# Stacked left-over rows for groups 4 to 15, held in the place of the split rows, and group 3's main feature matmuls ahead of group 1's second transform

## Chip, core and metric

The kernel runs on one core of one Trainium2 chip. The metric is the device time of one execution in microseconds (us), the median of three runs. A core has TensorE (PE: the matmuls; PEld: its weight loads), VectorE (DVE), ScalarE (ACT), GpSimd (POOL) and SyncE (SP), which issues most of the DMAs. Sixteen DMA engines carry out what the queues issue.

## What is computed

A spectral filter with a residual, and after it a bilinear gated layer with a residual. The change lies in the first half of the filter, the two-dimensional forward transform.

```python
def _A_ref(x, w_r, w_i):                     # x is 1 x 2048 x 640
    X = rfft2(x, axes=(-2, -1))
    X = X * (w_r + 1j * w_i)                 # w is 2048 x 321
    return irfft2(X, s=(S, D), axes=(-2, -1))

def _B_ref(x, w_gate, w_up, w_down):         # 640 -> 1728 -> 640
    g = einsum("bsd,df->bsf", x, w_gate)
    u = einsum("bsd,df->bsf", x, w_up)
    return einsum("bsf,fd->bsd", g * u, w_down)

x = A_x
h = x + _A_ref(_layernorm(x), A_w_r, A_w_i)
out = h + _B_ref(_layernorm(h), B_w_gate, B_w_up, B_w_down)
```

## The kernel before

The transforms are matmuls with constant tables. A first stage over 16 row tiles (to about 38 us) folds and normalises the rows and leaves the first transform in `s1` (four parts of 128 rows) and `rest` (128 left-over rows), both ordered by 16 groups of 128 columns. `rest_split` writes the left-over rows as a rounded high part (ACT, L281) and the remainder (DVE, L282) into `s1r`.

The second stage (about 40 to 111 us) is a loop over the 16 groups. For a group, `d_mm` makes the feature transform on PE: four main matmuls of full fp32 precision and then the left-over rows. Of a plain group these are six matmuls of 322 columns (high by high, high by low, low by high, for `re` and `im`). Of a group in `ST` they are four matmuls of 160 to 194 columns, whose stationary tile has 99 rows: the high rows, the low rows and the high rows again, 33 each, stacked. `d_out` copies the PSUM banks to `t` (ACT, L437 to L440). `s2_mm` makes the second transform into the PSUM tile `u`, of which there is one. `filt` multiplies by the filter (DVE, L455 to L458; the first three read `u`). `is2_mm` starts the inverse, and `is2_out` copies it away (ACT L506 and L517, DVE L524, POOL).

[...] `spread` writes 33 rows of `s1r` for a run of groups to `sfar` in DRAM (four DMAs, L422), and `stack` reads them back as 99 rows for two or three groups (two DMAs, of 66 and of 33 rows, L429). Groups 5 to 14 are stacked, by four stacks in two buffers (`dC`, `qt`) in turn; groups 0 to 4 and 15 are plain.

Each group also needs a load set: `load_wm` (the 128x256 tile `m` of the second transform from `in_mm_dram` L385, the 128x644 filter `wre` L386 and for even groups, which fetch it for two, `wim` L388) and `load_wi` (a second 128x256 tile L393). The tiles have three places by `g % 3`, so a set is issued three groups ahead, when the readers of its place are done.

The order is written out by hand (`manual_schedule`), each engine works in program order, and all the DMAs named here are issued by SP, one after another: one that has to wait holds up those behind it. In iteration `g`, the order is `s2_mm(g)`, `d_mm(g+2)`, `is2_mm(g-1)`, `filt(g)`, `load_wm(g+3)`, `d_out(g+2)`, `is2_out(g-1)`, `load_wi(g+2)`. Ahead of the loop stand the load sets of groups 0, 1 and 2, the spread of groups 5 to 9, and `d_mm` and `d_out` of groups 0 and 1. From about 111 us on come the inverse feature transform and the gated layer, on PE nearly without a gap.

Of the kernel before, what the change touches and what calls it, by code (L numbers as in the profile page):

```python
# [11 lines left out]
F32 = mybir.dt.float32  # L12
F32R = mybir.dt.float32r
# [3 lines left out]
P = 128  # L17
S, D, NF, FF = 2048, 640, 321, 1728
NT = S // P
NG = 16  # L20
# [4 lines left out]
RROWS = ((31, 1), (0, 1), (62, 2), (63, 2))  # L25
RWHERE = ((1, 0), (0, 0), (1, 160), (0, 160))
RW = (160, 194, 162, 162)
PLAIN, LAST = 5, 15
IPLAIN, IFAR = 6, 10
SUMS = 7  # L30
IPARTS = ((6, 4), (10, 3), (13, 3))
AGAIN = {0: (5, 3), 1: (8, 2, "qt"), 5: (10, 3), 7: (13, 2, "qt")}
NR = 4
AHEAD = 5
FOLDS = {0: (1, 2), 1: (3,), 2: (4,), 7: (9,), 9: (11,)}
# [11 lines left out]
def f32(ap):  # L47
    return ap.bitcast(F32)
# [29 lines left out]
def tile_spectral_glu(ctx: ExitStack, tc: tile.TileContext, x, wre, wim, wgu, wlast, wdown, wdlast,  # L78
# [6 lines left out]
    far = ctx.enter_context(tc.tile_pool(name="far", bufs=1, space=bass.MemoryType.DRAM))  # L85
# [13 lines left out]
    def bank(tag, bufs=2):  # L99
        return pools["y" if tag in ("im2", "ir2") else "a"].tile([P, 512], F32, tag=tag, name=tag, bufs=bufs)  # L100
# [10 lines left out]
    def wk(shape, name):  # L111
        return work.tile(shape, F32, tag="wk", name=name)
# [4 lines left out]
    def mmx(o, l, r, start, stop):  # L117
        nc.tensor.matmul(o, l, r, start=start, stop=stop, skip_group_check=True)  # L118
# [13 lines left out]
    def home(tag, shape, name, dt=F32):  # L132
        return keep.tile(shape, dt, tag=tag, name=name)

    def cut(t, o, *shape):
        v = t[:, o:o + int(np.prod(shape))]
        names = [f"d{i}" for i in range(len(shape))]
        return v.rearrange(f"p ({' '.join(names)}) -> p {' '.join(names)}", **dict(zip(names[1:], shape[1:])))
# [6 lines left out]
    s1r = home("wA", [P, 2, NG, P], "s1r", F32R)  # L145
# [127 lines left out]
    def s1_rest(t):  # L273
        act(at(rest, t), PS1[t][1][:, 0:P].rearrange("p (g m) -> p g m", g=32), AF.Copy)

    def s1_main(t, ps, a, b):
        act(view(s1, 4 * t + 2048 * a, [[2048, b - a], [64, 32], [1, 4]]),
            ps[:, a * P:b * P].rearrange("p (c g m) -> p c g m", c=b - a, g=32), AF.Copy)

    def rest_split(a, b):  # L280
        act(s1r[:, 0, a:b], rest[:, a:b], AF.Copy)  # L281
        tt(s1r[:, 1, a:b], rest[:, a:b], f32(s1r[:, 0, a:b]), op=OP.subtract)  # L282

    banks("y", "pinv")
# [30 lines left out]
    for t in range(NT):  # L315
        if t == 1:
            nc.gpsimd.dma_start(frall, frem)
        if t >= 1:
# [18 lines left out]
            if t < AHEAD - 1:  # L337
                s1_rest(t - 1)
                main = lambda: s1_main(t - 1, PS1[t - 1][0], 0, 4)
# [25 lines left out]
        else:  # L365
            scale_c(0)
            b2a, b2, b3a, a2, b3, a3, m, v = stats[0]
# [6 lines left out]
        s1_mm(t)  # L374
    s1_main(NT - 1, PS1[NT - 1][0], 2, 4)
    s1_rest(NT - 1)
    for a, b in ((0, 2), (2, PLAIN), (PLAIN, PLAIN + 5), (PLAIN + 5, 13), (13, 16)):
        rest_split(a, b)

    WM, WI = {}, {}  # L380

    def load_wm(g):
        m, w, j = mts[g % 3], wts[:, g % 3], g // 2 if g < NG - 2 else g - 7
        i = wts[:, 5 if j == 8 else 3 + j % 2]
        nc.sync.dma_start(m, mm[g, :, 0])  # L385
        nc.sync.dma_start(w, wre[g])  # L386
        if g % 2 == 0 or g >= NG - 2:
            nc.sync.dma_start(i, wim[j])  # L388
        WM[g] = (m, w, i)

    def load_wi(g):
        WI[g] = wis[g % 3]
        nc.sync.dma_start(WI[g], mm[g, :, 1])  # L393

    qm = home("qm", [P, 4, NT, P], "qm")
    qr = home("qr", [P, 2, NT, P], "qr", F32R)
    PD, T, PU, Y, PI = {}, {}, {}, {}, {}

    def parts(ps, main, rest):
        for k, (b, o, w, l, r) in enumerate(main):  # L400
            mmx(ps[b][:, o:o + w], l, r, k < 2, False)
        for k, (b, l, r) in enumerate(rest):
            mmx(ps[b][:, 0:NQ], l, r, False, k >= len(rest) - 2)

    def d_mm(g):
        ps = PD[g] = bank("re"), bank("im")
        where = ((1, 0), (0, 0), (1, 160), (0, 160))
        main = [(b, o, FW[c], s1[:, c, g], fmt[:, FOFF[c]:FOFF[c] + FW[c]]) for c, (b, o) in enumerate(where)]
        if g not in ST:
            parts(ps, main, [(b, s1r[:, k, g], frt[:, l, b]) for k, l in ((0, 0), (0, 1), (1, 0)) for b in range(2)])  # L410
            return
        parts(ps, main, [])
        for q, ((b, o), w) in enumerate(zip(RWHERE, RW)):
            a = 4 * NQ + sum(RW[:q])
            mmx(ps[b][:, o:o + w], ST[g][0:99, q], frall[0:99, a:a + w], False, q >= 2)

    ST = {}
    sfar = far.tile([4, 2, 33, LAST - PLAIN, P], F32, name="sfar")

    def spread(a, b):  # L420
        for q, (r, s) in enumerate(RROWS):
            nc.sync.dma_start(sfar[q, :, :, a - PLAIN:b - PLAIN].rearrange("l r g n -> r l g n"),  # L422
                              f32(s1r[r:r + 32 * s + 1:s, :, a:b]))

    def stack(g, n, tag="dC"):
        o = home(tag, [P, 4, n, P], "st", F32R)
        src = sfar[:, :, :, g - PLAIN:g - PLAIN + n].rearrange("q l r g n -> q (l r) (g n)")
        for a, b, r in ((0, 66, 0), (66, 99, 0)):
            nc.sync.dma_start(f32(o[a:b].rearrange("p q g n -> p q (g n)")),  # L429
                              src[:, r:r + b - a].rearrange("q r n -> r q n"))  # L430
        for i in range(n):
            ST[g + i] = o[:, :, i]

    def d_out(g):
        ps = PD[g]
        t = T[g] = wk([P, 2, NQ], "t")
        act(t[0:64, 0], ps[0][0:64, 0:NQ], AF.Copy)  # L437
        act(t[0:64, 1], ps[0][64:128, 0:NQ], AF.Copy)
        act(t[64:128, 0], ps[1][0:64, 0:NQ], AF.Copy)
        act(t[64:128, 1], ps[1][64:128, 0:NQ], AF.Copy)  # L440

    def s2_mm(g):
        if g >= NG - 2:
            ps = PU[g] = bank("re"), bank("im")
        else:
            PU[g] = pools["y"].tile([P, 2, 512], F32, tag="u", name="u", bufs=1)
            ps = PU[g][:, 0], PU[g][:, 1]
        for h in range(2):
            nc.tensor.matmul(ps[h][:, 0:NQ], WM[g][0][:, h], T[g][:, h], start=True, stop=True)  # L449
# [10 lines left out]
    def filt_half(g, h, alone=False):  # L460
        if h == 0:
            Y[g] = wk([P, 2, NQ], "y"), wk([P, 2, NQ], "us")
        y, us = (a[:, h] for a in Y[g])
        v, w, im = PU[g][h][:, 0:NQ], WM[g][1], WM[g][2]
        direct = lambda: tt(y, v, w[:, h], op=OP.mult)
        join = lambda: tt(y, y, us, op=OP.add)
        if alone:
            direct()
            nc.vector.scalar_tensor_tensor(us[0:64], v[64:128], -1.0, im[64:128, h], op0=OP.mult, op1=OP.mult)
            tt(us[64:128], v[0:64], im[0:64, h], op=OP.mult)  # L470
            return direct, join
        act(us[0:64], v[64:128], AF.Copy, scale=-1.0)
        act(us[64:128], v[0:64], AF.Copy)
        nc.gpsimd.tensor_tensor(us, us, im[:, h], op=OP.mult)
        return direct, join
# [55 lines left out]
        main(slice(0, 4))  # L531
        edges(nc.gpsimd)

    for g in range(3):
        load_wm(g)
        load_wi(g)
    spread(PLAIN, PLAIN + 5)
    d_mm(0)
    d_out(0)
    d_mm(1)  # L540
    d_out(1)
    for g in range(NG - 1):
        s2_mm(g)
        if g + 2 < NG:
            d_mm(g + 2)
        if g >= 5 and g in AGAIN:
            stack(*AGAIN[g])
        if g + 3 == NG:
            xt = home("big", [P, 2, 5, 2, 512], "xt", F32R)
            flat = xt[:, 1].rearrange("p k l n -> p (k l n)")  # L550
            irt, sirt = cut(flat, 0, 5, NQ), cut(flat, 5 * NQ, 4, 162)
            scrap, near = cut(flat, 2258, D), cut(flat, 2258 + D, 4, 4, P)
        if g == NG - 2:
            nc.gpsimd.dma_start(flat[:, 0:2258], irem)
        if g == NG - 2:
            s2_mm(g + 1)
            filt_half(g, 0, True)
            is2_out(g - 2)
        if g >= 1:
            is2_mm(g - 1)  # L560
        if g < NG - 2:
            filt(g)
        else:
            late = [filt_half(g, 1), filt_half(g + 1, 0), filt_half(g + 1, 1, True)]
            for f in (late[0][0], late[1][0], late[1][1], late[2][1]):
                f()
        if g + 3 < NG:
            load_wm(g + 3)
        if g + 2 < NG:
            d_out(g + 2)  # L570
        if g >= 1:
            if g != NG - 3:
                is2_out(g - 1)
            if g + 2 < NG:
                load_wi(g + 2)
        if g < 2:
            stack(*AGAIN[g])
        elif g == 2:
            spread(PLAIN + 5, LAST)
        if g == 6:  # L580
            nc.sync.dma_start(cit, ci)
            nc.sync.dma_start(imt, imain)
# [248 lines left out]
    for ts in (range(3), range(3, 6), range(6, 8)):  # L831
        n, t0 = len(ts), ts[-1] + 1
# [660 lines left out]
```

## Time and profile before

| | |
|---|---|
| median of 3 runs | 681.81 us (681.48 to 682.31) |
| the profiled execution | 682.02 us, its span 680.2 us |
| PE busy | 668.6 us, 98% of the span |
| DVE / ACT / POOL busy | 472.5 / 322.0 / 392.0 us |
| HBM read / written | 54.20 / 10.57 MB |

The span is what the trace covers; the execution's own time lies 1.8 us above it. Times in the rows are counted from the span's start. A busy share is an average over stages with different limits, so a change in one stage is read from the rows of that stage. A wait is put down to the event that came last in the record, which need not be the one that was waited for.

### The profile page before, as it was taken

To read this page: it belongs to the slowest core of one execution; us is meant where nothing else is said; L and a number is where in the kernel's file an instruction comes from. 1 tells how busy PE (TensorE), PEld (TensorE's weight loads), DVE (VectorE), ACT (ScalarE), POOL (GpSimd) and SP (SyncE) were. 2 spreads that over 40 slices of the span, in tenths; PEclk is the share of its full clock that TensorE was granted. 3 is DMA by queue.
4 is the path that set the end of the run, shared out by engine and by line. 5 is a ranking of instruction groups with operands and counts; after the bars stand their busy time and mean duration, and the time that the engine had idled before them with its cause. 6 is when DMAs were issued, how large, how long until landed. Compare 5 with 4: busy or idle time off the path is not lost.

```text
span 680.2 us, 10297 instructions
## 1 busy us (share of the span) xinstructions
PE 668.6 (98%) x3714; PEld 591.2 (87%) x3714; DVE 472.5 (69%) x966; ACT 322.0 (47%) x623; POOL 392.0 (58%) x376
## 2 busy tenths in 40 slices
PE   8999999999999999999999999999999999999997
PEld 8988888887888888888888889888888888888887
DVE  7968887787965958576767747854747575756654
ACT  6966665476534434352525336543434252524220
POOL 3101123642099787876987634199687878787610
PEclk9999999999999999999999999999999999999999
DMA  9537965502111102133242449201112121212003
GB/s 333 205 104 242 270 192 164 145 28 78 52 49 58 48 28 78 40 97 79 77 93 82 99 87 296 82 21 49 49 39 78 40 78 39 78 40 79 1 1 154
DMA packets 49085, 65.44 MB, mean 96 GB/s; under 512 B 24086, under 2 KB 31326, under 8 KB 48906
## 3 DMA queue, kind: packets, MB, share of 16 engines
q1 hardware_dynamic: 48314, 62.23, 29.7%
q0 software_dynamic: 288, 2.16, 0.9%
q8 instruction: 29, 0.48, 0.3%
q10 hardware_dynamic: 432, 0.39, 0.2%
q14 instruction: 22, 0.18, 0.1%
HBM read 54.20 MB, written 10.57 MB: 95 GB/s over the span
## 4 chain that ended last, share of the span: by engine, by line
PE 93%; DMA 3%; DVE 2%; ACT 1%; issue 1%; ACTq 0%; SPq 0%; DVEq 0%
PE e L118 50%; PE d L118 26%; PE eo L118 3%; PE u L449 3%; PE re L118 2%; PE im L491 2%; PE im L118 2%; PE y L118 2%; DMA tab<-in_fmain_dram 1%; PE im L251 1%; PE ir L491 1%; DMA x<-in_x_dram 1%; DMA cct<-in_cc_dram 1%; DMA wts<-in_wre_dram 0%; PE u L491 0%
## 5 line engine op out<-in xcount | busy, mean ns | idle before, releaser
L118 PE MATMUL e<-xt,wst 128*128 128x512 f32 x864 | 213.3, 391 | 0.7 <-ACT c L1076 0.7
L118 PEld LDWEIGHTS e<-xt,wst 128*128 128x128 f32 x864 | 159.8, 188 | 31.5 <-ACT c L1076 0.9
L1011 DVE TENSOR_TENSOR x<-d,x 128x320 f32<-128x320 f32 x280 | 123.4, 484 | 51.6 <-PE d L118 47.4
L118 PE MATMUL d<-wd,ht 128*128 128x320 f32 x832 | 143.6, 308 | 0.0
L118 PEld LDWEIGHTS d<-wd,ht 128*128 128x128 f32 x832 | 131.1, 188 | 7.6
L118 PE MATMUL e<-t,wst 128*128 128x512 f32 x360 | 94.3, 392 | 0.0
L925 POOL TENSOR_TENSOR wst<-raw,wst 128x1024 fp32r<-128x1024 f32 x23 | 55.5, 2411 | 66.3 <-ACT wst L924 55.8
L118 PEld LDWEIGHTS e<-t,wst 128*128 128x128 f32 x360 | 66.3, 188 | 12.6
L118 PE MATMUL d<-wt,ht 128*128 128x320 f32 x360 | 69.5, 310 | 0.0
L941 POOL TENSOR_TENSOR wst<-raw,wst 128x896 fp32r<-128x896 f32 (+1 forms) x46 | 65.1, 1439 | 3.3 <-ACT wst L936 3.3
L118 PEld LDWEIGHTS d<-wt,ht 128*128 128x128 f32 x360 | 57.3, 188 | 2.4
L1027 ACT ACTIVATE ht<-e 128x512 fp32r<-128x512 f32 x44 | 26.3, 598 | 47.5 <-DVE e L1090 23.3
L936 ACT ACTIVATE wst<-raw 128x896 fp32r<-128x896 f32 (+1 forms) x48 | 30.2, 676 | 31.7 <-POOL raw L930 30.9
L1066 ACT ACTIVATE h<-e 128x512 f32<-128x512 f32 x24 | 14.3, 596 | 64.2 <-PE e L118 64.2
L520 POOL CAST qr<-bits 1x128 fp32r<-1x128 f32 x15 | 4.2, 282 | 69.7 <-DVE qr L524 69.7
L986 DVE TENSOR_TENSOR x<-d,x 128x320 f32<-128x320 f32 x62 | 27.5, 485 | 23.2 <-PE d L118 22.9
L118 PE MATMUL e<-xt,wdir 128*128 128x512 f32 x180 | 42.3, 393 | 0.1
L627 ACT ACTIVATE wd<-draw 128x320 fp32r<-128x320 f32 (+1 forms) x30 | 15.7, 558 | 54.6 <-POOL draw L637 51.4
L1086 DVE TENSOR_TENSOR e<-e,h 128x512 f32<-128x512 f32 x24 | 16.8, 699 | 33.9 <-PE e L118 24.2
L118 PEld LDWEIGHTS e<-xt,wdir 128*128 128x128 f32 x180 | 33.4, 188 | 7.8 <-issue 0.6
L1030 DVE TENSOR_TENSOR ht<-e,ht 128x512 fp32r<-128x512 f32 x54 | 37.0, 686 | 1.6 <-ACT ht L1027 1.3
L606 POOL TENSOR_TENSOR wd<-draw,wd 128x640 fp32r<-128x640 f32 x8 | 12.5, 1580 | 40.8 <-ACT wd L605 40.8
(224 smaller groups left out, 1205.8 us busy)
## 6 DMA issues: line engine op xcount, KB each, us to landing
raw<-in_wgu_dram SPq DMA_DIRECT2D x24, 640.0 KB
draw<-in_wdown_dram SPq DMA_DIRECT2D x24, 320.0 KB
wts<-in_wre_dram SPq DMA_DIRECT2D x16, 322.0 KB
x<-in_x_dram SPq DMA_DIRECT2D x15, 320.5 KB
out_dram<-x SPq DMA_DIRECT2D x15, 320.0 KB
bits<-in_mm_dram SPq DMA_DIRECT2D x32, 128.0 KB
wts<-in_wim_dram SPq DMA_DIRECT2D x9, 322.0 KB
zfar<-zr SPq DMA_DIRECT2D x32, 80.0 KB
```

Source lines behind the costliest of these rows:

```text
L118: nc.tensor.matmul(o, l, r, start=start, stop=stop, skip_group_check=True)
L449: nc.tensor.matmul(ps[h][:, 0:NQ], WM[g][0][:, h], T[g][:, h], start=True, stop=True)
L491: nc.tensor.matmul(out, y[:, h, a:b], inv(g, h), start=n == 0, stop=n == len(ys) - 1)
L627: act(o[:, 0, a:a + n], src, AF.Copy)
L925: ptt(wa[:, 1], stage[:, 0:1024], f32(wa[:, 0]), op=OP.subtract)
L936: act(ws[:, 0, o:o + b - a], stage[:, a:b], AF.Copy)
L941: ptt(ws[:, 1, o:o + b - a], stage[:, a:b], f32(ws[:, 0, o:o + b - a]), op=OP.subtract)
L986: tt(xv, ps[b][:, 0:320], xv, op=OP.add)
L1011: tt(xv, o, xv, op=OP.add)
L1027: act(hop[:, a, 0], src, AF.Copy)
L1030: engine.tensor_tensor(hop[:, a, 1], src, f32(hop[:, a, 0]), op=OP.subtract)
L1086: tt(ob, ob, h1, op=OP.add)
```

## The change

Groups 4 to 15 are stacked. The first spread covers groups 4 to 8, the second 9 to 15. There are five stacks: groups 4 to 6 (`dC`), 7 and 8 (`qt`), 9 to 11 and 12 to 14 (both inside `s1r`, in the place of the split rows that have been spread), and 15 (`qt`). They are issued ahead of the loop and in iterations 0, 3, 5 and 7. The split of groups 9 to 15 moves from ahead of `d_out(0)` to behind `d_out(1)` on ACT and behind `filt(0)` on DVE. Group 2's load set is issued behind the first spread instead of ahead of it. On PE the main matmuls of group 3 move from behind `s2_mm(1)` to ahead of it.

```diff
-PLAIN, LAST = 5, 15
+PLAIN, MID = 4, 9
...
-AGAIN = {0: (5, 3), 1: (8, 2, "qt"), 5: (10, 3), 7: (13, 2, "qt")}
+AGAIN = {0: (7, 2, "qt"), 3: (9, 3, 0), 5: (12, 3, 1), 7: (15, 1, "qt")}
...
-    def rest_split(a, b):
+    def rest_high(a, b):
         act(s1r[:, 0, a:b], rest[:, a:b], AF.Copy)
+
+    def rest_low(a, b):
         tt(s1r[:, 1, a:b], rest[:, a:b], f32(s1r[:, 0, a:b]), op=OP.subtract)
...
-    for a, b in ((0, 2), (2, PLAIN), (PLAIN, PLAIN + 5), (PLAIN + 5, 13), (13, 16)):
-        rest_split(a, b)
+    for a, b in ((0, 2), (2, PLAIN), (PLAIN, MID)):
+        rest_high(a, b)
+        rest_low(a, b)
...
-    qr = home("qr", [P, 2, NT, P], "qr", F32R)
...
-    def d_mm(g):
-        ps = PD[g] = bank("re"), bank("im")
+    def d_mm(g, half=None):
+        if half != 1:
+            PD[g] = bank("re"), bank("im")
+        ps = PD[g]
...
+        if half == 1:
+            main = []
+        if half == 0:
+            parts(ps, main, [])
+            return
...
-    sfar = far.tile([4, 2, 33, LAST - PLAIN, P], F32, name="sfar")
+    sfar = far.tile([4, 2, 33, NG - PLAIN, P], F32, name="sfar")
...
-    def stack(g, n, tag="dC"):
-        o = home(tag, [P, 4, n, P], "st", F32R)
+    def stack(g, n, tag):
+        if tag in (0, 1):
+            o = s1r[:, tag, PLAIN:NG].rearrange("p (q n) m -> p q n m", q=4)
+        else:
+            o = home(tag, [P, 4, n, P], "st", F32R)
...
-    for g in range(3):
+    for g in range(2):
         load_wm(g)
         load_wi(g)
-    spread(PLAIN, PLAIN + 5)
+    spread(PLAIN, MID)
+    load_wm(2)
+    load_wi(2)
+    stack(PLAIN, 3, "dC")
     d_mm(0)
     d_out(0)
     d_mm(1)
     d_out(1)
+    rest_high(MID, NG)
     for g in range(NG - 1):
         s2_mm(g)
         if g + 2 < NG:
-            d_mm(g + 2)
-        if g >= 5 and g in AGAIN:
+            d_mm(g + 2, 1 if g == 1 else None)
+        if g == 0:
+            d_mm(3, 0)
+        if g >= 2 and g in AGAIN:
             stack(*AGAIN[g])
...
-        if g < 2:
+        if g == 0:
             stack(*AGAIN[g])
-        elif g == 2:
-            spread(PLAIN + 5, LAST)
+            rest_low(MID, NG)
+            qr = home("qr", [P, 2, NT, P], "qr", F32R)
+        elif g == 1:
+            spread(MID, NG)
```

In the rows of order, a name ahead of the arrow is what is written: `bits` holds `m` and the second 128x256 tile, `wts` the filter. On SP's queue behind the last row tile, and from group 2's load set to the second stack, there stood before:

```order
L385 DMA bits<-in_mm_dram 128x256
L386 DMA wts<-in_wre_dram 128x644
L388 DMA wts<-in_wim_dram 128x644
L393 DMA bits<-in_mm_dram 128x256
L422 DMA sfar<-s1r 33x2x640 x4
L385 DMA bits<-in_mm_dram 128x256
L386 DMA wts<-in_wre_dram 128x644
L429 DMA st<-sfar 66x4x384
L429 DMA st<-sfar 33x4x384
```

The same stretch of SP's queue now:

```order
L431 DMA sfar<-s1r 33x2x640 x4
L388 DMA bits<-in_mm_dram 128x256
L389 DMA wts<-in_wre_dram 128x644
L391 DMA wts<-in_wim_dram 128x644
L396 DMA bits<-in_mm_dram 128x256
L441 DMA st<-sfar 66x4x384
L441 DMA st<-sfar 33x4x384
L388 DMA bits<-in_mm_dram 128x256
L389 DMA wts<-in_wre_dram 128x644
```

Group 2's four loads moved behind the spread, and the stack of three groups moved ahead of group 3's two loads.

Further down SP's queue, from group 5's loads over the second spread to group 6's first load, there stood before:

```order
L385 DMA bits<-in_mm_dram 128x256
L386 DMA wts<-in_wre_dram 128x644
L393 DMA bits<-in_mm_dram 128x256
L422 DMA sfar<-s1r 33x2x640 x4
L385 DMA bits<-in_mm_dram 128x256
```

and on the same stretch now:

```order
L431 DMA sfar<-s1r 33x2x896 x4
L388 DMA bits<-in_mm_dram 128x256
L389 DMA wts<-in_wre_dram 128x644
L396 DMA bits<-in_mm_dram 128x256
L441 DMA s1r<-sfar 66x4x384
L441 DMA s1r<-sfar 33x4x384
L388 DMA bits<-in_mm_dram 128x256
```

The spread is larger (896 columns for 640) and stands ahead of group 5's loads, where it stood behind them; a stack of three groups, which used to come after group 7's loads, now stands ahead of group 6's. Likewise the next stack of three (groups 12 to 14) now stands ahead of group 8's loads.

On PE, from the last left-over matmul of group 2 to the first of group 3, there stood before (`u` is written by the second transform, `tab` names the main matmuls, `frt` those of the left-over rows):

```order
L118 MATMUL im<-frt,s1r 128x322
L449 MATMUL u<-t,bits 128x322 x2
L118 MATMUL im<-tab,s_88 128x160
L118 MATMUL re<-tab,s_88 128x193
L118 MATMUL im<-tab,s_88 128x161
L118 MATMUL re<-tab,s_88 128x161
L118 MATMUL re<-frt,s1r 128x322
```

and now:

```order
L118 MATMUL im<-frt,s1r 128x322
L118 MATMUL im<-tab,s_88 128x160
L118 MATMUL re<-tab,s_88 128x193
L118 MATMUL im<-tab,s_88 128x161
L118 MATMUL re<-tab,s_88 128x161
L461 MATMUL u<-t,bits 128x322 x2
L118 MATMUL re<-frt,s1r 128x322
```

The four main matmuls of group 3 moved past the second transform of group 1.

## Rows read from the trace of the kernel before

**Rows 1.** The page's part 4: the chain that ended last, by engine.

```profile
PE 93%; DMA 3%; DVE 2%; ACT 1%; issue 1%; ACTq 0%; SPq 0%; DVEq 0%
```

**Rows 2.** PE in order of time: start, duration, what, idle time before and releaser.

```profile
46.68 1.32 PE L449 MATMUL u<-t,bits 128*128 128x322 f32 x4 [0.78 <-ACT t L438]
...
48.88 0.42 PE L118 MATMUL re<-frt,s1r 128*128 128x322 f32 x1
...
49.87 0.60 PE L491 MATMUL ir<-bits,y 128*65 128x128 f32 x4
...
51.20 1.25 PE L449 MATMUL u<-t,bits 128*128 128x322 f32 x4
...
57.79 0.35 PE L118 MATMUL im<-frt,st 99*128 99x160 f32 x1
...
58.31 0.60 PE L491 MATMUL ir<-bits,y 128*65 128x128 f32 x4
...
60.01 1.32 PE L449 MATMUL u<-t,bits 128*128 128x322 f32 x4 [0.20 <-PE im L491]
...
68.56 1.32 PE L449 MATMUL u<-t,bits 128*128 128x322 f32 x4 [0.21 <-PE im L491]
```

**Rows 3.** ACT in order of time: the first copy of groups 2, 3 and 5.

```profile
45.78 0.43 ACT L437 ACTIVATE t<-re 64x322 f32<-64x322 f32 x1 [1.05 <-PE re L118]
...
49.92 0.43 ACT L437 ACTIVATE t<-re 64x322 f32<-64x322 f32 x1 [2.34 <-PE re L118]
...
58.57 0.43 ACT L437 ACTIVATE t<-re 64x322 f32<-64x322 f32 x1 [1.05 <-PE re L118]
```

**Rows 4.** DVE in order of time: the filter's first step for groups 1 and 3.

```profile
48.04 0.83 DVE L455 TENSOR_TENSOR y<-u,wts 128x644 f32<-128x644 f32 x1 [0.76 <-PE u L449]
...
57.38 0.83 DVE L455 TENSOR_TENSOR y<-u,wts 128x644 f32<-128x644 f32 x1
```

**Rows 5.** Lines 281 and 282, the split: durations in ns, minimum/median/maximum.

```profile
L281 ACT ACTIVATE s1r<-rest x5: 416/506/722, 38.9 to 40.7; 128x384 fp32r<-128x384 f32 x3, 128x256 fp32r<-128x256 f32 x1, 128x640 fp32r<-128x640 f32 x1
L282 DVE TENSOR_TENSOR s1r<-rest,s1r x5: 426/553/826, 39.4 to 41.6; 128x384 fp32r<-128x384 f32 x3, 128x256 fp32r<-128x256 f32 x1, 128x640 fp32r<-128x640 f32 x1
```

**Rows 6.** The loop's end: DVE and PE in order of time.

```profile
105.06 0.41 DVE L524 TENSOR_TENSOR qr<-ir,qr 64x256 fp32r<-64x256 f32 x1
...
105.56 0.62 PE L491 MATMUL ir<-bits,y 128*65 128x128 f32 x4 [0.34 <-PE im L449]
```

**Rows 7.** SP in order of time: the first spread, the first and the third stack.

```profile
41.27 2.55 SPq L422 DMA_DIRECT2D sfar<-s1r  x4
...
46.65 0.76 SPq L429 DMA_DIRECT2D st<-sfar  x2
...
67.05 0.76 SPq L429 DMA_DIRECT2D st<-sfar  x2
```

**Rows 8.** What SP's queue waited for: us in total, times, longest.

```profile
SPq L429 <- DMA sfar<-s1r: 1.4, 1, 1.4
```

**Rows 9.** Stretches: length, busy us of each engine, granted clock, DMA busy share, GB/s.

```profile
42.00:46.00 4.00, 3.89 (x23) 3.19 (x21) 2.25 (x4) 2.82 (x7) 0.00 (x0) 1.00 0.66 195
47.00:53.00 6.00, 6.00 (x39) 5.40 (x38) 4.15 (x7) 3.54 (x9) 0.10 (x1) 1.00 0.82 192
66.00:67.00 1.00, 1.00 (x11) 1.00 (x10) 0.97 (x2) 0.07 (x1) 0.69 (x2) 1.00 0.01 3
68.00:73.00 5.00, 4.79 (x33) 4.18 (x32) 4.56 (x7) 3.54 (x9) 0.73 (x2) 1.00 0.90 199
73.00:76.00 3.00, 3.00 (x22) 2.72 (x21) 2.35 (x4) 1.89 (x5) 0.74 (x2) 1.00 1.05 373
```

**Rows 10.** DMA issues between 40 and 66 us: count and KB (1024 bytes) of one.

```profile
wts<-in_wre_dram SPq DMA_DIRECT2D x5, 322.0 KB
bits<-in_mm_dram SPq DMA_DIRECT2D x9, 128.0 KB
st<-sfar SPq DMA_DIRECT2D x1, 396.0 KB
```

## The prediction

> **What bounds the kernel now.** I read the chain of the page first: 93% of what ended last is PE [rows 1]. After 111 us PE works on in its own order, so a shift of the second stage's end should reach the end of the kernel one to one. Then the second stage in order of time. A second transform starts at 60.01 us and the one two groups later at 68.56 us [rows 2]: 8.55 us for two groups, with 0.20 us of idle PE ahead of it. The reader is to see a loop in that: a second transform, the feature matmuls of the group two further on, their copies on ACT, the filter on DVE, which frees the one tile `u`, and the next second transform. Two such loops, of the even and the odd groups, run interleaved. Last I read the DMA engines by stretches [rows 9]. From 42 us they are 66 to 105% busy and run dry only at 66 to 67 us, at 3 GB/s. That the engines are a resource with little to spare in this stage decides the forecast.
>
> **The matmuls.** The left-over rows of plain group 3 take from 48.88 to 49.87 us, 0.99 us, those of stacked group 5 from 57.79 to 58.31 us, 0.52 us [rows 2]. Two groups change, 4 and 15: 2 x 0.47 = 0.94 us less PE work. The main matmuls of group 3 go into the 0.78 us that PE idles ahead of 46.68 us [rows 2]. Together this caps the gain at 1.72 us. Most of it is not on the path:
>
> - *Group 1's filter gets later.* DVE is done with group 0's filter at 48.04 - 0.76 = 47.28 us [rows 4]. The subtract of groups 9 to 15, 896 columns, now stands there. 640 columns take 826 ns, 384 take 553 ns [rows 5], so 1.07 ns a column and 826 + 256 x 1.07 = 1.10 us. Group 1's filter starts at 48.38 and not 48.04 us. From a filter's start to the next second transform is 60.01 - 57.38 = 2.63 us [rows 2, 4], so group 2's starts at 51.01 us and not 51.20 us [rows 2]: -0.19 us.
> - *The copies of group 4 start sooner.* From the first left-over matmul to the first copy it is 49.92 - 48.88 = 1.04 us in a plain group, 58.57 - 57.79 = 0.78 us in a stacked one [rows 2, 3]: -0.26 us. Group 4's second transform, and with it the even loop, is then at -0.45 us. The odd loop gains a little more and waits for nobody.
> - *The rounding of groups 9 to 15 on ACT.* By the same slope, 722 + 256 x 0.84 = 0.94 us [rows 5]. It falls into the 1.05 us in which ACT idles before 45.78 us [rows 3], so nothing; without that cover it would cost the 0.94 us once, on DVE's subtract.
> - *Group 15.* The first inverse matmul of group 13 at 105.56 us follows a DVE step that ends at 105.47 us [rows 6], behind filter work that comes from the even loop, not group 15's matmuls. I take 0 of its 0.47 us; the bounds are 0 and -0.47 us.
>
> So with no new wait the kernel ends at -0.45 us.
>
> **The DMA queue.** This is where the change moves most. Before, group 2's loads were done long before the stage. Now 128 + 322 + 322 + 128 = 900 KB of them stand behind the first spread (`wim` has the shape of `wre`) [rows 10]. The second spread has 7 groups for 5, and the stack of groups 9 to 11 stands ahead of group 6's loads, that of 12 to 14 ahead of group 8's. A stack of three groups is 396 + 198 = 594 KB, half as much again as its 66-row part [rows 10].
>
> What a stack costs is not its bytes at full rate. The third one is issued at 67.05 us into an empty queue [rows 7]; between 68 and 73 us the engines move 199 GB/s at 90% busy, and from 73 us on, with only loads left, 373 GB/s [rows 9]. The first stack shows the same, 192 GB/s at 47 to 53 us [rows 9]. Some of the loads behind it pass in that time on engines that it does not use, but a load is complete only when its last share has landed, behind the stack. So for the load next in line a stack of three costs 5.0 us; the lower bound is its 0.61 MB at 373 GB/s, 1.6 us, the upper bound the 6 us from issue to the end of the slow stretch. I take 5.0, since two stacks show it. The spread bears on this too: at 42 to 46 us, with almost only spread traffic, 66% of the engines' time is busy [rows 9].
>
> The Trainium skill says in DMA: Bandwidth & Descriptors, section "Why a DMA increments its semaphore by 16 and not by 1", that a DMA uses the largest number of engines up to 16 that divides its slowest dimension; 33 and 66 rows would use 11 of 16, or 69%, and a load of 128 rows all 16. The trace's 66% agrees with that.
>
> **Group 6's tile `m`.** The first spread has landed when the first stack is issued at 46.65 us, after a wait of 1.4 us for it [rows 7, 8]; it starts 0.1 us sooner now, since one group less is split ahead of it (128 columns, 0.14 us on DVE). So from 46.5 us. Before, the queue then moved everything up to group 7's loads by 66.1 us [rows 9], 19.6 us. The new queue up to group 6's `m` differs by: group 2's set instead of group 6's (both even, 0); group 7's 578 KB left out, -0.59 MB / 373 = -1.6 us; a stack of three more, +5.0; group 6's 128 KB, +0.35; the spread by two groups more, 0.27 MB at 195 GB/s [rows 9], +1.4; and the slow start of the first stack, which had nothing ahead of it, about -0.4. That is 24.35 us, so `m` lands at 70.85 us. Without a wait group 6's second transform would start at 68.56 - 0.45 = 68.11 us. It now starts at some 70.95 us, **+2.39 us** against before. Bounds for the whole 5.60 MB ahead of it: at 373 GB/s it lands at 61.5 us, no wait; at 195 GB/s at 75.2 us, +6.7 us.
>
> **Group 4's stacked tile.** 46.5 + 2.5 (group 2's set at 373 GB/s) + 5.0 = 54.0 us. It is needed at 51.01 + 48.88 - 46.68 = 53.2 us [rows 2]. PE waits 0.8 us there, which turns -0.45 into +0.4 us for groups 3 to 5; group 6's wait then swallows it.
>
> **Group 8's tile `m`.** After group 6's `m` the queue holds the rest of group 6's set (772 KB, 2.1 us), group 7's set (1.6 us), the stack of groups 12 to 14 (5.0 us) and `m` (0.35 us): 70.85 + 9.05 = 79.9 us. Due is 70.95 + 8.55 = 79.5 us. Another 0.5 us with the wait's own 0.1 us; between -0.5 (no wait) and +1.5 us if the stack takes 4 or 6 us. After it only one group is left to stack, and the loads have their lead again.
>
> **Sum.** +2.39 + 0.5 = +2.9 us on the even loop, carried to the end. On the profiled execution that is 682.02 + 2.9 = 684.9 us, against the median of 681.81 us, which is what is predicted on, 684.7 us. Stacks now live in `s1r`; a place there is written only after the second spread has left it, which the order of SP's queue gives anyway, so that costs nothing by itself.
>
> **The rivals.**
>
> *No wait* (not slower): the queue keeps up, since in the old one stack traffic had dry times and now always has work ahead. It decides if a stack among other traffic costs under some 2.2 us, 70.85 - 68.05 = 2.8 us less than I take. For it speaks that 1.6 us is its price at full rate, against it both slow stretches [rows 9]. Time 681.81 - 0.45 = 681.4 us. The skill's fit in DMA: Bandwidth & Descriptors, section "Anatomy of one DMA", made for DMAs issued from GpSimd, is 2.0 us plus the bytes at 436 GB/s. As an estimate by that rule 5.60 MB would be through 14.8 us after 46.5 us, with no wait; the trace's 192 and 199 GB/s disagree.
>
> *Small waits*: group 4's wait and less than 1.8 us at group 6, so the end lies between -0.4 and +1.36 us, about 682.4 us. A stack would cost between 2.2 and 4 us.
>
> *Heavy waits*: a stack costs 6 us, all in the queue. Group 6's `m` lands 1 us later and group 8's 2 us later: +2.9 + 1 + 1 = +4.9 us, 686.7 us. For it speaks that every stack now has loads on both sides.
>
> *Faster by the whole cap*: PE as the bound, -1.72 us, 680.1 us. Against it stands the 0.20 us of idle PE in each pair of groups [rows 2].
>
> **How the numbers follow.** The forecast, both waits at +1.4 to +4.2 us, gets 0.50, heavy waits 0.19, small waits 0.16, no wait 0.12, the cap 0.03. A measurement of this kernel tells some 0.2%, 1.36 us, from no change: slower 0.69, same 0.28, faster 0.03. The range goes from the case without a wait, 681.3 us, to just over heavy waits, 687.2 us; the rest of the heavy case and the cap stay out.
>
> **What would show it.** Right: PE idle ahead of group 6's second transform for 2 us or more, released by a DMA of `m`, and a short one ahead of group 8's; DMA over 85% busy without a dry stretch from 42 to about 80 us; left-over matmuls of group 4 of 0.52 us, perhaps after a wait for `st`. Wrong: a DMA stretch near 0% before 70 us, or second transforms 8.55 us apart from group 2 on, both of which would mean the no-wait case. A granted clock under 1.00 behind a wait would add to the loss; no row shows an idle PE this long.

## The result

The changed kernel takes 684.1 us (median of 6 runs, 683.9 to 685.67) where the kernel before takes 681.8 us (681.33 to 682.8) on the same chip: a ratio of 1.0037, 95% interval 1.0025 to 1.005, so 2.3 us more. The profiled execution is one of the longer ones, 685.67 us with a span of 683.9 us. A second one, taken later of the same kernel (label e10 below), took 684.62 us with a span of 682.9 us.

| | before | after | after, second trace |
|---|---|---|---|
| execution, us | 682.02 | 685.67 | 684.62 |
| group 2's second transform starts | 51.20 | 50.64 | 50.91 |
| group 4's | 60.01 | 61.57 | 61.48 |
| group 6's | 68.56 | 72.11 | 71.71 |
| group 8's | 77.11 | 80.66 | 80.27 |
| first inverse matmul of group 13 | 105.56 | 108.92 | 108.52 |

The time is lost in two steps, at groups 3 to 4 and at group 6, and it stays lost. The page's chain that ended last, which answers [rows 1], shows that transfers have come into it: 8% DMA where it was 3%.

```profile
PE 79%; DMA 8%; DVE 6%; ACT 2%; SPq 2%; issue 1%; POOL 1%; DVEq 0%; ACTq 0%; POOLq 0%
```

PE in order of time, after, against [rows 2] (start, duration, what, idle time before and releaser):

```profile
50.64 1.32 PE L461 MATMUL u<-t,bits 128*128 128x322 f32 x4 [0.63 <-DVE us L469]
...
55.32 0.31 PE L118 MATMUL im<-frt,st 99*128 99x160 f32 x1 [2.21 <-DMA st<-sfar]
...
61.57 1.32 PE L461 MATMUL u<-t,bits 128*128 128x322 f32 x4 [0.29 <-PE im L503]
...
72.11 1.32 PE L461 MATMUL u<-t,bits 128*128 128x322 f32 x4 [2.28 <-DMA bits<-in_mm_dram]
...
80.66 1.32 PE L461 MATMUL u<-t,bits 128*128 128x322 f32 x4 [0.35 <-DVE us L469]
```

There are two long waits of PE for a transfer: 2.21 us for group 4's stacked rows and 2.28 us for group 6's `m`. Ahead of group 8 there is none. The second trace has the same two, 1.85 and 1.97 us.

The chain of waits between 50 and 75 us (start, duration, what) tells what group 6's `m` was waiting for. The kernel before has no transfer in its chain between 44 and 82 us.

```profile
49.34 9.68 DMA st<-sfar
59.02 0.02 issue
59.04 0.81 SPq L431
59.85 0.04 issue
59.90 5.26 DMA sfar<-s1r
65.15 0.02 issue
65.17 0.03 SPq L441
65.20 0.04 issue
65.24 0.32 SPq L441
...
66.03 5.93 DMA bits<-in_mm_dram
71.97 0.14 issue
72.11 1.32 PE u L461 x4
```

Read from the top: the stack of groups 7 and 8 lands; the last two parts of the second spread can then be issued; the last one lands in DRAM 5.26 us after its issue; only then may SP issue the stack of groups 9 to 11, and right behind it, at 66.03 us, `m`. Three landings stand one behind the other, 9.68 + 5.26 + 5.93 = 20.87 of the 22.77 us. While SP stands ahead of that stack, the transfer engines have little to do, and more loads for later groups stand behind it in SP's queue. The stretches of after (length, busy us of each engine, clock, DMA share, GB/s), against [rows 9]:

```profile
62.00:65.00 3.00, 3.00 (x23) 2.75 (x22) 2.72 (x5) 1.53 (x5) 0.73 (x2) 1.00 0.80 267
65.00:67.00 2.00, 2.00 (x14) 1.67 (x13) 1.34 (x2) 1.94 (x5) 0.00 (x0) 1.00 0.23 48
67.00:72.00 5.00, 2.83 (x24) 2.63 (x22) 4.15 (x6) 3.58 (x9) 1.09 (x4) 1.00 0.94 237
```

From 65 to 67 us the engines are 23% busy, 3 to 5 us before PE stands still for want of `m` (from 69.83 us).

The first link of the chain is not one of data: the spread reads nothing that the stack of groups 7 and 8 writes. In all the traces of this case SP's DMAs use eight semaphores in turn, and from 38 to 110 us none is issued before the one eight places ahead of it has landed. So at most eight are under way, and one that lands late holds up the eighth behind it, whatever that one moves. What SP waited for in the changed kernel (us in total, times, longest) shows it: group 4's `wim` (L391) waited for the stack of groups 4 to 6, and the parts of the second spread (L431) for group 3's loads and for the stack of groups 7 and 8.

```profile
SPq L391 <- DMA st<-sfar: 2.3, 1, 2.3
...
SPq L431 <- DMA st<-sfar: 1.5, 1, 1.5
...
SPq L431 <- DMA wts<-in_wre_dram: 0.8, 1, 0.8
...
SPq L431 <- DMA bits<-in_mm_dram: 0.5, 1, 0.5
```

No run here changes the number of eight, so its share of the loss is not measured.

### The profile page after: what moved, and what is told of

It is laid out like the page before. It is cut to its first block, busy times and chain, and to the rows that moved or that the text cites. A ratio compares the mean times of both kernels' runs of the same rounds, so it can differ in the third digit from the quotient of the medians.

```text
span 683.9 us, 10290 instructions
## 1 busy us (share of the span) xinstructions
PE 667.3 (98%) x3710; PEld 589.8 (86%) x3710; DVE 471.9 (69%) x965; ACT 322.0 (47%) x622; POOL 391.9 (57%) x376
## 4 chain that ended last, share of the span: by engine, by line
PE 79%; DMA 8%; DVE 6%; ACT 2%; SPq 2%; issue 1%; POOL 1%; DVEq 0%; ACTq 0%; POOLq 0%
PE e L118 45%; PE d L118 23%; DMA x<-in_x_dram 2%; PE eo L118 2%; PE u L461 1%; DMA st<-sfar 1%; PE y L118 1%; PE im L251 1%; DMA z<-zfar 1%; PE re L118 1%; DMA xt<-ifar 1%; PE im L118 1%; PE im L503 1%; DMA bits<-in_mm_dram 1%; DMA raw<-in_wgu_dram 1%
```

## The experiments

The theory T: the waits come from the order in which SP issues, since loads stand behind stacks that have to wait themselves. The rivals: R1, the bytes alone fill the transfer engines, and the waits only change place; R2, group 4's wait alone sets the end and the later one inherits it; R3, no transfer but the order on PE or the new place of the stacks costs the time. "Before" is the kernel before, run together with it on the same chip.

| edit of the changed kernel | median, us | before | ratio (95%) |
|---|---|---|---|
| e1: group 2's set ahead of the spread | 682.61 | 681.59 | 1.0023 (1.0011 to 1.0035) |
| e2: stack of groups 9 to 11 behind the loads | 685.21 | 681.59 | 1.0052 (1.0038 to 1.0066) |
| e8: all three later stacks behind the loads | 684.03 | 681.69 | 1.0037 (1.0025 to 1.0048) |
| e3: e1 and e8 together | 681.68 | 681.59 | 0.9999 (0.999 to 1.0007) |
| e9: e3, and the stack of 7 and 8 later | 681.51 | 681.60 | 1.0001 (0.9991 to 1.0011) |
| e11: only the stack of 7 and 8 later | 684.53 | 681.60 | 1.0049 (1.0033 to 1.0065) |
| e5: the stack of 9 to 11 twice | 692.34 | 681.59 | 1.0151 (1.0138 to 1.0164) |
| e4: PE move undone | 684.32 | 681.69 | 1.005 (1.0037 to 1.0063) |
| e6: the kernel before with the PE move only | 681.68 | 681.69 | 1.0 (0.9992 to 1.0009) |
| e7: e3 with the PE move undone | 681.66 | 681.69 | 1.0004 (0.9995 to 1.0012) |

### Group 2's set ahead of the spread (e1)

```diff
-    spread(PLAIN, MID)
     load_wm(2)
     load_wi(2)
+    spread(PLAIN, MID)
     stack(PLAIN, 3, "dC")
```

> The changed kernel with one edit: the filter data of group 2 is issued ahead of the first spread again, not between that spread and the first stack of left-over rows (groups 4 to 6). Theory T (what SP issues in a row sets it: group 4's rows wait behind set 2, and group 6's m waits behind a stack that itself waits for the second spread): group 4's wait on TensorE goes from 2.2 us to below 0.5, the second spread and group 6's m follow 1 to 2 us sooner, group 6's wait of 2.3 us shrinks to about 1; total 682.3 to 683.3 us. Rival R2 (group 4's wait alone sets the end, the later one only inherits it): 681.4 to 681.9 us. Rival R3 (no transfer at all, the order on TensorE or the place of the stacks costs the time): 684.1 us, unchanged.

Measured 682.61 us. PE's wait for group 4's rows is gone, group 6's `m` is issued at 62.80 instead of 66.03 us, and what is left are two smaller waits for `m`. PE in order of time:

```profile
54.86 1.26 PE L461 MATMUL u<-t,bits 128*128 128x322 f32 x4
...
68.97 1.32 PE L461 MATMUL u<-t,bits 128*128 128x322 f32 x4 [1.42 <-DMA bits<-in_mm_dram]
...
77.80 1.32 PE L461 MATMUL u<-t,bits 128*128 128x322 f32 x4 [0.63 <-DMA bits<-in_mm_dram]
```

The total and group 4's wait are as T had them; `m` comes 3.2 us sooner, where 1 to 2 us were expected, and the wait at group 8 was not. R2 falls in its strict form, since 1.0 us of loss remains without any wait of group 4. R3 falls too: 1.3 of the 2.3 us go away with four transfers moved.

### One stack behind the loads (e2)

```diff
-        if g >= 2 and g in AGAIN:
+        if g >= 2 and g in AGAIN and not g in (3,):
             stack(*AGAIN[g])
...
         elif g == 1:
             spread(MID, NG)
+        if g in (3,):
+            stack(*AGAIN[g])
```

> The changed kernel with one edit: the second stack of three groups' rows (7 to 9 in after's numbering of its issue, the one that is issued ahead of group 6's m) goes to the end of its pass of the loop, behind the filter data of group 6 and the imaginary inverse matrix of group 5. Theory T (issue order on SP): TensorE's wait of 2.3 us for group 6's m is gone, group 4's wait of 2.2 us stays as it was, perhaps a small wait at group 7 or 8; total 682.3 to 683.3 us. Rival R1 (the bytes alone fill the transfer engines): the wait only moves to group 7 or 8, total 683.5 us or more. Rival R2 (group 4's wait sets the end): 684.1 us. Rival R3 (no transfer): 684.1 us.

(The stack meant is that of groups 9 to 11.) Measured 685.21 us, no faster than the changed kernel with its 684.1 us (the two were not run together): T's number is missed. Group 6's `m` is now issued at 61.32 us and nobody waits for it. But group 8's `m`, issued at 69.26 us behind the stack of groups 12 to 14 (67.11 us), is late instead. PE and the stretches behind it:

```profile
79.74 1.50 PE L461 MATMUL u<-t,bits 128*128 128x322 f32 x4 [1.88 <-DMA bits<-in_mm_dram]
...
85.45 1.25 PE L461 MATMUL u<-t,bits 128*128 128x322 f32 x4
```

```profile
80.00:82.00 2.00, 2.00 (x8) 1.56 (x8) 0.72 (x1) 0.00 (x0) 0.41 (x1) 0.69 0.96 329
82.00:84.00 2.00, 2.00 (x10) 2.00 (x9) 1.92 (x4) 0.00 (x0) 0.00 (x0) 0.50 0.93 227
```

The wait moved to another place, as R1 said. It also drew a second loss: TensorE's granted clock fell to 0.50, the lower of its two levels, and from group 8's second transform to group 9's it took 5.71 us where the changed kernel takes 84.71 - 80.66 = 4.05 us. Whether it is bytes (R1) or again a load behind a stack (T), the next two runs tell apart.

### All later stacks behind the loads, without and with e1's edit (e8, e3)

```diff
-        if g >= 2 and g in AGAIN:
+        if g >= 2 and g in AGAIN and not g in (3, 5, 7):
             stack(*AGAIN[g])
...
+        if g in (3, 5, 7):
+            stack(*AGAIN[g])
```

> The changed kernel with one edit: the stacks that open passes 3, 5 and 7 of the loop (groups 9 to 11, 12 to 14, and 15) all go to the ends of those passes, behind the loads; group 2's data stays behind the first spread as in the changed kernel. Theory T (a load that is issued behind a stack is late, whichever stack it is; the run that moved only the stack of groups 9 to 11 passed the wait on to group 8's load, behind the stack of groups 12 to 14): no wait for filter data at all, group 4's wait of 1.7 to 2.2 us stays, no fall of TensorE's clock between 60 and 110 us; total 682.6 to 683.4 us. Rival R1 (bytes fill the engines): a wait of over 1 us for filter data at some group from 6 to 12, 684 us or more.

> The changed kernel with both edits: the filter data of group 2 ahead of the first spread, and the stacks that start passes 3, 5 and 7 of the loop at the ends of those passes, behind the loads. The bytes moved are the same. Theory T (issue order on SP): no wait of TensorE for a transfer between 45 and 110 us is above 0.5 us, and the end comes as the sum without waits gave it, 681.2 to 681.6 us. Rival R1 (bytes): waits stay in another place, 683 us or more. Rival R3 (no transfer): 684.1 us.

With both edits (e3) the same bytes take 681.68 us, the time of the kernel before. In its trace the only wait of PE for a transfer above 0.63 us between 45 and 110 us is the one for group 4's rows, 0.76 us, and the loop ends at 105.48 us, as in [rows 6]:

```profile
53.88 0.31 PE L118 MATMUL im<-frt,st 99*128 99x160 f32 x1 [0.76 <-DMA st<-sfar]
...
105.48 0.62 PE L503 MATMUL ir<-bits,y 128*65 128x128 f32 x4 [0.70 <-PE im L461]
```

R1 and R3 fall with that: neither the traffic as such nor the place in `s1r` nor PE's order costs 2.3 us. The 0.76 us is over T's bound of 0.5 us, and the total 0.1 us over its range. (The 0.63 us that PE idles ahead of group 2's second transform is put down to the same DMA in this trace, but that transform reads no stacked rows, and in the changed kernel the same 0.63 us ends with DVE.)

With the stacks alone (e8) the median is 684.03 us, no better than the changed kernel and 0.6 us above T's range. R1's total of 684 us or more is met, its wait of over 1 us for filter data is not. Its executions lie far apart, 682.33 to 685.38 us. The profiled one, 685.38 us, waits 2.35 us for group 4's rows, and there too the clock fell behind the wait:

```profile
55.37 0.31 PE L118 MATMUL im<-frt,st 99*128 99x160 f32 x1 [2.35 <-DMA st<-sfar]
...
84.60 1.32 PE L461 MATMUL u<-t,bits 128*128 128x322 f32 x4 [0.52 <-DMA bits<-in_mm_dram]
```

```profile
55.00:57.00 2.00, 1.63 (x11) 1.66 (x12) 0.30 (x1) 0.92 (x3) 0.00 (x0) 0.80 0.93 207
57.00:59.00 2.00, 2.00 (x9) 1.75 (x8) 0.42 (x1) 1.93 (x5) 0.00 (x0) 0.50 0.76 186
```

From the first stacked matmul of group 4 (55.37 us) to group 4's second transform at 62.82 us it took 7.45 us; the changed kernel, with the same wait and the full clock, took 61.57 - 55.32 = 6.25 us. A second trace of the same kernel (e12) was taken to see it without that:

> The kernel whose three later stacks go behind the loads, once more for a second profiled execution: the first one lost 1.2 us to a fall of TensorE's clock behind group 4's wait of 2.35 us. Where the clock does not fall, theory T expects a total of 683.4 to 684.1 us with group 4's wait of 2 to 2.4 us as the only one above 0.5 us.

This execution took 682.09 us, 1.3 us less than expected at the least. Group 4's wait is itself 1 us shorter in it:

```profile
54.46 0.31 PE L118 MATMUL im<-frt,st 99*128 99x160 f32 x1 [1.31 <-DMA st<-sfar]
```

So the late stacks do take the wait for `m` away, in both traces but for 0.52 us at group 9. What they leave is group 4's wait, 1.3 or 2.4 us long from one execution to the next, with a fall of the clock in one of the two. Why the same program has that wait in two sizes these runs don't tell. Which of the two waits costs more stays open: by the medians e1, without group 4's wait, gains 1.5 us and e8, without the wait at group 6, 0.1 us, but the one trace of e8 at full clock takes 2.0 us less than the changed kernel's median.

### The changed kernel once more (e10)

> The changed kernel itself once more, for a second profiled execution nearer to its median than the first (685.67 against 684.1 us). Theory T: both waits of TensorE, for group 4's rows and for group 6's m, are in it again, together 3 to 4.5 us; the first trace's surplus of 1.6 us over the median is the size of these waits and nothing behind 110 us. Rival R2 (group 4's wait alone sets the end): the wait for group 6's m is absent where the total is 684.

684.62 us, with waits of 1.85 and 1.97 us, 3.8 us together: T's range, and against R2. Its chain reads like the one above, 10.74 us for the stack of groups 7 and 8, 5.39 us for the spread, 5.79 us for `m`. Of the first trace's surplus of 1.05 us over this one, 0.4 us lie ahead of 110 us; the rest lies behind it, where nothing was expected, and its cause stays open.

### What makes group 4's rows late (e9, e11)

```diff
         if g == 0:
-            stack(*AGAIN[g])
             rest_low(MID, NG)
...
         elif g == 1:
+            stack(*AGAIN[0])
             spread(MID, NG)
```

On top of e3 (e9), and on the changed kernel alone (e11):

> The kernel with group 2's data ahead of the first spread and the later stacks behind the loads, with one more edit: the stack of groups 7 and 8 (396 KB) moves from the end of pass 0 to pass 1, behind that pass's loads and ahead of the second spread. If the wait of 0.8 us for group 4's rows that is left there comes from sharing the transfer engines with this stack, it is gone, nothing waits for a transfer any more, and the total is 0.5 to 0.8 us under that kernel: 680.9 to 681.2 us where the kernel before takes 681.6. If the wait comes from the loads that stay behind group 4's stack: 681.7 us, unchanged.

> The changed kernel with one edit: the stack of groups 7 and 8 moves from the end of pass 0 to pass 1, ahead of the second spread. If group 4's rows are late because this stack shares the engines with them: group 4's wait falls from 2.2 us to below 0.7. If they are late because group 2's 0.9 MB are queued ahead of them: it stays at 1.5 us or more. The second spread and with it the stack of groups 9 to 11 and group 6's m go later by up to 2 us, so that wait grows in exchange; total 683.5 to 685 us.

In e9 the wait for group 4's rows is gone. From the issue of its second part to landing, their stack takes 7.39 us in e3, by the chain:

```profile
46.35 7.39 DMA st<-sfar
```

In e9 that part is issued at 46.51 us and lands at 53.18 us, by its semaphore, after 6.67 us; PE takes the rows up at 53.32 us. The next stack, each of whose two parts is the eighth DMA behind one of these, goes out from 51.51 us on, its second part at 53.20 us:

```profile
53.32 0.31 PE L118 MATMUL im<-frt,st 99*128 99x160 f32 x1
```

```profile
51.51 2.00 SPq L441 DMA_DIRECT2D st<-sfar  x2
```

That the 0.7 us come from the stack of groups 7 and 8 is not shown. In e1 SP's queue has the same order as in e3 up to there, with that stack in its old place, and there is no wait either:

```profile
53.01 0.35 PE L118 MATMUL im<-frt,st 99*128 99x160 f32 x1
```

In e11, where group 2's set still stands behind the spread, the wait is 1.34 us, between the two expectations. Of the changed kernel, e2, e5 and e8, whose queues are the same up to there, six traces have 1.31 to 2.35 us, so e11 can't be told from them. What the traces do show is the set: in all eight with group 2's set behind the spread this wait is 1.31 to 2.35 us, and in the four with the set ahead of it (e1, e3, e7, e9) it is 0.76 us once and else absent. The waits for `m` of groups 6 and 8 are 1.39 and 0.85 us in e11, and the total, 684.53 us, lies in the range given. But the second spread comes sooner than in the changed kernel's trace, at 54.76 and not 56.11 us, and group 6's wait is smaller; the opposite was expected.

The wait-free e9 should have shown 0.5 to 0.8 us of gain. It takes 681.51 us where the kernel before takes 681.60, and its interval goes from -0.6 to +0.7 us. In its trace the loop ends 0.66 us before [rows 6], and the inverse feature transform starts at 110.91 us and not 111.59 us; of these 0.68 us the span shows 0.3 (679.9 against 680.2 us). One place where some of it goes can be seen: PE then waits for `xt`, for 0.2 us in the kernel before, and in e9 for 0.5 us (in total, times, longest):

```profile
PE eo L118 <- DMA xt<-ifar: 0.5, 1, 0.5
```

### The price of a stack (e5)

```diff
             stack(*AGAIN[g])
+            if g == 3:
+                stack(*AGAIN[g])
```

> The changed kernel with one edit: the stack that is issued ahead of group 6's m is issued twice in a row (the second writes the same rows again; extra work, nothing is left out). Theory T: the price of one stack ahead of group 6's m, by the prediction's 5.0 us, stands before that load once more, so its wait grows from 2.3 to about 6 to 7 us and the total to 688 to 689 us. Rivals R2 (group 4's wait alone) and R3 (no transfer): 684.1 us.

692.34 us, where 688 to 689 us were expected. Group 6's wait is 6.56 us, as expected, and its second transform starts 4.05 us later than in the first trace of the changed kernel, 4.45 us later than in the second:

```profile
76.16 2.49 PE L461 MATMUL u<-t,bits 128*128 128x322 f32 x4 [6.56 <-DMA bits<-in_mm_dram]
```

```profile
76.00:78.00 2.00, 1.84 (x4) 1.27 (x5) 0.00 (x0) 0.00 (x0) 0.00 (x0) 0.50 1.00 360
```

What the expectation left out is the clock, at 0.50 when PE goes on at 76 us: group 7's second transform follows at 82.93 us, 6.77 us later and not 4.05 us, another 2.7 us. How the 4 us come about is not a full queue either: SP's queue waited 4.1 us for the first copy to land before it issued the second one, presumably since both write the same place, which no run here tests.

```profile
SPq L441 <- DMA s1r<-sfar: 5.8, 3, 4.1
```

So this run measures the landing time of a stack ahead of `m`: 5.15 us in its chain, from the issue of the second part, while SP stands still for 4.1 of them.

### The PE move (e4, e6, e7)

```diff
-            d_mm(g + 2, 1 if g == 1 else None)
-        if g == 0:
-            d_mm(3, 0)
+            d_mm(g + 2)
```

This edit on the changed kernel is e4, on e3 it is e7; e6 is the kernel before with the reverse of it.

> The changed kernel with the TensorE move alone undone: all feature matmuls of group 3 stand again behind the second transform of group 1. Theory T: group 2's second transform starts about 0.3 to 0.5 us later (before's order: it was 51.20 us there and 50.64 us in the changed kernel), but the wait of 2.2 us for group 4's stacked rows behind it shrinks by as much; total 684.1 us within 0.3. Rival R3 (the order on TensorE costs the time): 681.5 to 682 us.

> The kernel with group 2's data ahead of the first spread and the later stacks behind the loads, with the TensorE move undone as well. That kernel still waits 0.8 us for group 4's stacked rows, so the move's 0.3 to 0.5 us has no place to show: theory T gives 681.7 us within 0.3, unchanged, with a wait for group 4's rows of 0.3 to 0.5 us. If the move is worth its full amount in spite of that wait: 682.0 to 682.2 us.

> The kernel before with the TensorE move alone added; left-over rows, stacks and loads stay as they were before the change. Theory T: group 2's second transform starts when the filter of group 1 is done, 0.3 to 0.5 us earlier than 51.20 us, and nothing behind it waits for a transfer, so the total falls by 0.2 to 0.5 us against the kernel before, to 681.1 to 681.4 us where that is 681.6. Rival R3 (the order on TensorE costs the time): 683 us or more.

All three are unchanged: 684.32 us against the 684.1 us of the changed kernel (not run together), 681.66 us where e3 has 681.68, and 681.68 us where the kernel before has 681.69. For e6 0.2 to 0.5 us of gain were expected; a gain of 0.2 us can't be told from none. In e7 group 4's rows are not waited for at all, where 0.3 to 0.5 us were expected. The trace of e6 has group 2's second transform at 50.99 us, 0.21 us earlier than in [rows 2]. It is not more because group 3's main matmuls keep PE busy until 46.93 us, when the second transform of group 1 starts, which started at 46.68 us before:

```profile
46.93 1.25 PE L456 MATMUL u<-t,bits 128*128 128x322 f32 x4
...
50.99 1.32 PE L456 MATMUL u<-t,bits 128*128 128x322 f32 x4 [0.60 <-DVE us L464]
```

## Why the prediction came out as it did

The forecast, slower by 2.9 us with 684.7 us predicted, met 684.1 us (2.3 us). Its cause, PE standing still for group 4's rows and above all for group 6's `m` behind a stack, is what the traces show and what e3 takes away. Its terms are not all right, and two errors cancel, group 6's wait too small and group 8's too large; that the total comes so close is in part luck.

- **The small terms.** Right. The subtract of 896 columns took 1.08 us (predicted 1.10) and the rounding 0.95 us (0.94), hidden on ACT. Group 2's second transform gained more than the 0.19 us predicted, 0.29 and 0.56 us; from group 0's second transform to it, it is 8.37 us in both traces and was 8.70 us before, so 0.33 us is the change's and the rest is where the stage starts.
- **Group 4's stacked tile.** The wait is right in kind and too small: the tile is needed at 53.1 us as predicted, and lands at 55.2 us and not at 54.0. The failed term is the stack's price of 5.0 us. By the semaphores, from the first part's issue to the second's landing, it took 8.8 us behind group 2's set (46.39 to 55.18 us), and 6.3 to 7.7 us with that set ahead of the spread (e1, e3, e7, e9). The first stack of the kernel before took 7.2 us too (46.65 to 53.81 us), more than the 5.0 us read from [rows 9].
- **Group 6's `m`.** Predicted at +2.39 us, measured at +3.55 and +3.15 us. The step that failed is the sum over the queue in bytes. It gave the two groups more of the second spread 1.4 us for their bytes and a stack 5.0 us of a busy queue, and no term for the time in which SP stands still: 5.1 us from 52 to 59 us, in the four waits shown above for DMAs eight places ahead, and 2.6 us ahead of the stack alone (62.61 to 65.24 us), for the spread. The chain is three landings in series, and from 65 to 67 us the engines are 23% busy. From the stack's issue to the landing of `m` it took 6.7 us (65.24 to 71.97 us), 5.35 us in the sum. That `m` still landed only 1.1 us later than the 70.85 us forecast is no proof of the sum, which counts as a busy queue what was in part SP's waiting.
- **Group 8's `m`.** Predicted +0.5 us, measured nothing: group 8's start is 3.55 us later than before, as group 6's is. `m` landed at 80.05 us by its semaphore (79.9 predicted), but it became due 0.8 to 1.2 us later than predicted, and was there. The place is a real one: where group 6's wait is smaller or gone, group 8 waits 0.58 us (e4), 0.63 us (e1), 0.85 us (e11) and 1.88 us (e2).
- **The end.** A shift of the second stage was to reach the end one to one. +3.36 us at the loop's end is +3.7 us in the span, +2.96 us is +2.7 us: right within 0.35 us. In the other direction e9's 0.68 us arrived only as 0.3 us.
- **What would show it.** Of the signs given, group 6's wait, a wait for `st` and the 0.5 us of group 4's left-over matmuls (55.32 to 55.81 us) came; the short wait ahead of group 8 and "over 85% busy without a dry stretch" did not. A nearly dry stretch before 70 us was named as a sign of the no-wait case. It turned out to go with the wait, since a queue that stands still feeds nobody.
- **The rivals.** No wait: its order exists, but is another one (e3, e9), and there the -0.45 us predicted for it can't be seen in the total. Heavy waits: its price of 6 us for a stack is nearer to what was measured than 5.0 us, but its wait at group 8 did not come. The clock, named as a possible addition, stayed at 1.00 in both traces of the changed kernel.

## What to carry to other kernels

A load that is issued behind a DMA which must wait for a round trip inherits the whole round trip, however empty the transfer engines are; so place a spread and its read-back behind the loads that fall due next, and here the loss was gone with the same bytes. In these traces the eighth DMA behind a late one waits as well, though it moves other data. Cost such a queue by the chain of issues and landings, and only then by bytes; a transfer engine that goes idle shortly before a wait points at the queue and not at the bandwidth. Where two such loads are late, mend both: moving one stack only handed the wait to the load behind the next one.

## What the hardware showed beside that

TensorE's granted clock fell to 0.50 behind waits of 1.88 us (e2) and 2.35 us (e8) and within one of 6.56 us (e5, 0.73 from 74 to 76 us), and this added 1.7, 1.2 and 2.7 us to them. It did not fall behind 2.28 and 2.21 us in the changed kernel, whose stretch after the wait has 1.00:

```profile
72.00:74.00 2.00, 1.90 (x9) 1.60 (x10) 0.53 (x1) 0.00 (x0) 0.38 (x1) 1.00 1.01 357
```

The length of the wait alone does not decide it, since 1.88 us had the fall and 2.28 us had not. The Trainium skill says in TensorE: Matmul & The Clock Gate, section "Part 1: The HAM clock gate (the "warmup" mystery)", that the clock is at half when the engine has been idle, and that the moment at which work brings it up again varies from run to run. That all three falls go to 0.50 agrees with the first; why one wait has a fall and another has not, no run here shows.

The variants of the changed kernel also scatter more. Fifteen executions of the kernel before lie between 681.0 and 682.49 us; six of e8 between 682.33 and 685.38 us, twelve of e1 between 681.9 and 685.84 us, and of two traces of e8 one has a wait of 2.35 us where the other has 1.31 us. Waits of PE are not all of it: eleven executions of e9, whose trace has none for these transfers, lie between 680.42 and 683.98 us.
